# A long convolution with a gate: stores of a_u on two queues, sums in place, and another order of filter steps and halo copies

## The chip, the cores and the metric

The kernel runs on one core of a Trainium2 chip. The core has five engines, each with an instruction stream of its own: TensorE (PE) for matrix products, VectorE (DVE), ScalarE (ACT), GpSimd (POOL) and SyncE (SP), which here only issues DMAs. An engine runs its instructions in the order in which they were written and waits where data or a buffer isn't ready. What counts is the device time of one execution in microseconds (us): the median of three runs.

## What is computed

```
h = (relu(pos_emb @ w1) @ w2) * exp(-0.01 * n)          # filter, 12800 x 128
u = x * v                                               # 4 x 12800 x 128
y = irfft(rfft(u, 25600) * rfft(h, 25600))[:, :12800]   # a causal convolution along the sequence
z = x * y
gate = sigmoid(sum over k < 5 of conv_w[k] * z shifted by 4 - k)
out  = (gate * (z @ w_val)) @ w_out
```

Batch 4, sequence 12800, 128 channels, 64 features of the filter, all in float32 (some weights arrive as float64 and are narrowed on the chip).

## The kernel before, in words

The sequence is split as J * N1 * N2 = 2 * 100 * 64, and the transforms into a part over N1 and one over N2. The program has three stages, and two tensors in device memory lie between them: `a_u` (the transform of u over N1) and `c_y` (the product, transformed back over N2).

**Stage one** (L204 to L412) runs over the 64 values of n2. For each, `fetch` (L293) loads one tile of x and v, 100 rows of 8 KiB, as three DMAs of 64, 32 and 4 rows (the table `PARTS`). The tiles form a ring: four of the general buffers `ld0` to `ld3`, two of its own (`xv6`, `xv7`), and from the end of the filter's first part until 48 tiles are fetched also `ld4` and `ld5`. `product` (L313) multiplies x by v on DVE. For a pair of n2, `prep` (L320) then forms sums and differences: two operations of 1024 columns into the second half of the tile (L326, L327) and, for each n2, two of 512 into tiles `us` and `ud` of two buffers each (L334). PE multiplies them by the table `fsd` into `fp` (L379), ACT copies `fp` into `st` (L380, four buffers), and `st` goes to `a_u` as three stores: 64 and 32 rows from ACT's queue (L386), 4 rows from SP's, one n2 later (`flush`, L397). A pair's tiles are handed back to the ring by `release` inside `prep`, as soon as DVE has formed the sums of the odd n2, and `fetch` follows at once.

Between these steps a generator `filt` computes the filter's transform `ag`, in three parts: 16 times two steps that turn and multiply the positions (L228 to L242), 32 steps of PE with a copy by ACT (`ap`, L256 to L262), and 26 steps with a rotation by ACT and DVE (`fk`, L269 and L270), a product and a copy (L280, L282). A table of costs spreads the steps over the first 0.87 of stage one: the parts get 25.6, 28.8 and 22.9 of 77.3, which is 18.4, 20.7 and 16.5 n2.

Stage two (L440 to L540) reads `a_u`, multiplies by the filter and writes `c_y`. The change doesn't touch it.

**Stage three** runs over 32 groups of four n2, each a step `t` of four quarters `r`. In each quarter PE sums and turns rows of `c_y` (`sd`, L595; `tp`, L609); ACT copies `sd` into `sd_sb` (L602) and part of `tp` into `dif` (L611); DVE forms `yr` from `tp` and `dif` (L619, L620); POOL multiplies by x into `ext` (L622). For the group two behind, DVE adds one tap of the gate per quarter (`gt`, L637); the first tap is ACT's (`tap(t + 1, 0)`, L634, in the last quarter), the sigmoid too (`sg`, L641, last quarter), and, for every fourth group, also the copy of the last rows of the former `ext` into the new one (`fill_halo`, L576, last quarter; behind it the copy of `tails` for the last four groups of a half). PE's products `v_ps` and `o_ps` and ACT's copy `o_sb` (L664) complete the output.

**DMA counters.** The program gives every DMA that SP or ACT issues one of eight counters in turn, `DMAHW0` to `DMAHW7`, which count when it has landed; those of GpSimd have eight others, `DMASW0` to `DMASW7`. An issue waits until the DMA that had its counter before has landed. An engine that waits so holds everything behind it.

## Time and profile before

| | us |
|---|---|
| median of three runs | 1182.41 (1181.82 to 1184.42) |
| profiled execution | 1177.74 |
| its span, first to last instruction | 1176.0 |
| PE busy | 1027.8 (87%) |
| DVE busy | 992.6 (84%) |
| POOL busy | 679.7 (58%) |
| ACT busy | 622.6 (53%) |

All times of rows below come from the profiled execution. Issuing a DMA isn't counted as busy time, nor is waiting on a counter, so ACT's 53% leaves out what its queue of stores costs it. The mean granted clock of PE is 0.953. In a view by windows, each engine has the time it was busy in the window and, in brackets, its instructions; then come PE's clock, the share of the sixteen DMA engines that was busy, and GB/s. In a row of a group, the numbers behind the first bar are busy time and mean length (ns), behind the second the idle time ahead of these instructions and what ended it. ACTq and SPq are the DMA issues of ACT and SP.

### The profile page before, as it was taken

What the parts mean: (1) busy time and instruction counts of PE and PEld (TensorE: products, weight loads), DVE (VectorE), ACT (ScalarE), POOL (GpSimd) and SP (SyncE); (2) the same over time, 40 slices, a digit from 0 to 9 for tenths busy, and PEclk for the clock granted to TensorE, in tenths of its full rate; (3) what the DMA queues carried; (4) which work ended last, traced back from release to release, by engine and by line L of the source; (5) the groups of instructions that cost most, each with busy time, mean ns of one, the idle gap of its engine ahead of it and who ended that gap; (6) DMA issues with size and microseconds to landing.
All of it is one profiled execution on the core that took longest, in us unless ns stands there. A gap on an engine that the chain in (4) does not pass through costs nothing. (4 is left out here: it accounts for less than half of the span.)

```text
span 1176.0 us, 19204 instructions
## 1 busy us (share of the span) xinstructions
PE 1027.8 (87%) x6968; PEld 479.7 (41%) x6968; DVE 992.6 (84%) x1146; ACT 622.6 (53%) x1000; POOL 679.7 (58%) x290
## 2 busy tenths in 40 slices
PE   3767788967675799999999999988999999999986
PEld 1333345534341344444444444333444444444432
DVE  6678886659986799999999999718999999999996
ACT  1233366667774244444444444346676767676763
POOL 1000000000000699999999999928889898898880
PEclk9789889888989799999999999999999999999999
DMA  8889898875879789989999989787787777687622
GB/s 253 289 312 321 287 336 323 310 254 203 307 277 323 260 300 307 311 305 311 309 311 310 314 307 306 245 284 291 272 304 260 282 276 295 263 312 259 236 85 112
DMA packets 81384, 329.98 MB, mean 281 GB/s; under 512 B 11812, under 2 KB 13036, under 8 KB 62092
## 3 DMA queue, kind: packets, MB, share of 16 engines
q1 hardware_dynamic: 38512, 196.90, 50.1%
q10 hardware_dynamic: 42204, 130.02, 28.0%
q0 software_dynamic: 576, 1.84, 0.6%
q8 instruction: 57, 0.93, 0.3%
q14 instruction: 35, 0.29, 0.1%
HBM read 197.64 MB, written 131.07 MB: 280 GB/s over the span
## 5 line engine op out<-in xcount | busy, mean ns | idle before, releaser
L622 POOL TENSOR_TENSOR ext<-yr,xr 128x400 f32<-128x400 f32 x120 | 303.2, 2528 | 40.5 <-DVE yr L620 38.3
L637 DVE SCALAR_TENSOR_TENSOR gt<-ext,cw,gt 128x1600 f32<-128x1600 f32 x128 | 240.7, 1881 | 0.8 <-ACT gt L634 0.8
L380 ACT COPY st<-fp 128x1024 f32<-128x1024 f32 x128 | 128.7, 1027 | 174.9 <-PE fp L379 66.7
L484 ACT COPY c_sb<-c_ps 128x1024 f32<-128x1024 f32 x100 | 101.4, 1014 | 201.7 <-PE c_ps L479 194.8
L479 PE MATMUL c_ps<-va,ld 64*64 64x512 f32 x1600 | 194.1, 594 | 0.0
L468 DVE TENSOR_TENSOR va<-z_ps,h_sb 128x2048 f32<-128x2048 f32 x50 | 114.6, 2291 | 49.7 <-ACT h_sb L452 32.9
L513 POOL TENSOR_TENSOR va<-va,vb 128x1024 f32<-128x1024 f32 x50 | 118.6, 2373 | 45.6 <-DVE vb L468 45.5
L198 POOL DMA_DIRECT2D ld<-a_u x4 | 2.7, 683 | 240.6 <-DMA a_u<-st 240.6
L379 PE MATMUL fp<-us,fsd 64*128 64x512 f32 x256 | 87.2, 763 | 62.3 <-ACT st L380 35.5
L656 PE MATMUL o_ps<-gd,wout 128*128 128x400 f32 x256 | 112.4, 521 | 19.2 <-DVE gd L651 11.2
L595 PE MATMUL sd<-ld,inv 128*64 128x512 f32 x512 | 124.8, 605 | 2.0 <-ACT sd_sb L602 1.0
L522 POOL TENSOR_TENSOR va<-va,vb 128x1024 f32<-128x1024 f32 x50 | 119.6, 2392 | 0.0
L521 POOL TENSOR_TENSOR vc<-vc,vd 128x1024 f32<-128x1024 f32 x50 | 119.0, 2379 | 0.0
L462 PE MATMUL z_ps<-ld,ld 64*64 64x512 f32 x800 | 111.3, 606 | 7.4 <-DMA a_u<-st 4.0
L479 PEld LDWEIGHTS c_ps<-va,ld 64*64 64x64 f32 x1600 | 73.7, 135 | 101.2 <-issue 100.9
L602 ACT COPY sd_sb<-sd 128x512 f32<-128x512 f32 x128 | 76.1, 595 | 72.2 <-PE sd L595 55.5
L468 DVE TENSOR_TENSOR vb<-z_ps,h_sb 128x2048 f32<-128x2048 f32 x50 | 114.0, 2280 | 0.0
L646 PE MATMUL v_ps<-ext,wval 128*128 128x400 f32 x256 | 107.1, 500 | 0.0
L479 PE MATMUL c_ps<-vc,ld 64*64 64x512 f32 x800 | 98.2, 604 | 3.6 <-ACT c_sb L484 3.6
L609 PEld LDWEIGHTS tp<-ident,sd_sb 128*128 128x128 f32 x512 | 58.3, 140 | 75.8 <-PE sd L595 49.5
L609 PE MATMUL tp<-ident,sd_sb 128*128 128x128 f32 x512 | 79.9, 280 | 3.7 <-DVE yr L620 2.6
L619 DVE TENSOR_TENSOR yr<-tp,dif 128x204 f32<-128x204 f32 x128 | 45.9, 358 | 42.0 <-ACT dif L611 40.8
(85 smaller groups left out, 1560.6 us busy)
## 6 DMA issues: line engine op xcount, KB each, us to landing
c_y<-c_sb ACTq DMA_DIRECT2D x100, 512.0 KB
ld<-a_u SPq DMA_DIRECT2D x48, 1024.0 KB
a_u<-st ACTq DMA_DIRECT2D x64, 512.0 KB
ld<-c_y SPq DMA_DIRECT2D x64, 512.0 KB
xr<-in_xt_dram SPq DMA_DIRECT2D x32, 800.0 KB
out_dram<-o_sb ACTq DMA_DIRECT2D x32, 800.0 KB
ld<-in_xv_dram SPq DMA_DIRECT2D x46, 512.0 KB
a_u<-st ACTq DMA_DIRECT2D x64, 256.0 KB
```

The costliest lines, as they stand in the source:

```text
L380: nc.scalar.copy(out=st[:, c], in_=fp.rearrange("k j e -> k (j e)"))
L462: nc.tensor.matmul(out=z[half[h], c], lhsT=wk[half[c], 0, half[h]], rhs=a2[half[c], h, j], start=True, stop=True)
L468: nc.vector.tensor_tensor(out, z.rearrange("p (b d) -> p b d", d=D).unsqueeze(1).to_broadcast([128, n, B, D]), h_sb.unsqueeze(2).to_broadc ...
L479: nc.tensor.matmul(out=c_ps[half[m], h], lhsT=wk[half[h], 1 + c, half[m]], rhs=vt[half[h], c].rearrange("p b d -> p (b d)"), start=(i == 0 ...
L513: nc.gpsimd.tensor_tensor(va[:, 0:2], va[:, 0:2], vb[:, 0:2], op=ALU.add)
L521: nc.gpsimd.tensor_tensor(vc, vc, vd, op=ALU.add)
L522: nc.gpsimd.tensor_tensor(va[:, 2:4], va[:, 2:4], vb[:, 2:4], op=ALU.add)
L595: nc.tensor.matmul(out=sd[c * N2:(c + 1) * N2], lhsT=inv[:, c], rhs=rows_in[s, c][:, r * B * D:(r + 1) * B * D], start=True, stop=True)
L609: nc.tensor.transpose(out=tp[:, b], in_=t[:, b], identity=ident)
L622: nc.gpsimd.tensor_tensor(e[:, r0 + r], yr, xr, op=ALU.mult)
L637: nc.vector.scalar_tensor_tensor(gt, rows(t, k), cw[:, k:k + 1], gt, op0=ALU.mult, op1=ALU.add)
L656: nc.tensor.matmul(out=o_ps, lhsT=wout, rhs=gd, start=True, stop=True)
```

## The change

Five things are changed.

1. The 32-row and 4-row stores of `a_u`, and six loads of tables, are issued by GpSimd. ACT keeps the 64-row store.
2. The sums `us` and `ud` are written into the first half of the tile that they come from (for the even n2 its first, for the odd n2 its second 512 columns), where PE reads them.
3. The tiles of a pair are handed back, and the next fetched, behind the stores of the odd n2 and no longer in `prep`; the ring has one more tile, `xv8`, so it has seven to nine.
4. The filter's parts are due evenly over 15, 18 and 27 n2 from n2 = 2 on.
5. In stage three the first tap moves from the last quarter to the second, `fill_halo` to the first quarter of the next step, and the copy of `tails` to its third.

```
-        ring += [(6, p1.tile([128, 4 * BD], F32, name="xv6")), (7, p1.tile([128, 4 * BD], F32, name="xv7"))]
+        ring += [(6, p1.tile([128, 4 * BD], F32, name="xv6")), (7, p1.tile([128, 4 * BD], F32, name="xv7")),
+                 (8, p1.tile([128, 4 * BD], F32, name="xv8"))]
         for i, (_, t) in enumerate(ring):
-            (nc.vector, nc.gpsimd)[i in (2, 5)].memset(t, 0.0)
+            (nc.vector, nc.gpsimd)[i in (2, 4, 6)].memset(t, 0.0)
...
             for c, op in enumerate((ALU.add, ALU.subtract)):
-                w = p1.tile([128, BD], F32, name="us" if c == 0 else "ud", bufs=US)
+                w = srcs[c][:, 0, n % 2]
                 nc.vector.tensor_tensor(w, srcs[c][:, 1, 0], srcs[c][:, 1, 1], op=op)
                 out.append(w)
             if n % 2 == 1:
-                release()
-                fetch()
+                using.append(list(pair))
+                pair.clear()
                 if n + 1 < N2:
                     product(ahead.pop(0))
...
+        def release():
+            for i, t, _ in using.pop(0):
+                if i not in (4, 5) or fetched[0] < BACK:
+                    ring.append((i, t))
+            fetch()
...
                 if n == 8:
-                    nc.scalar.dma_start(out=dft, in_=t_dft)
+                    nc.gpsimd.dma_start(out=dft, in_=t_dft)
...
-                for k0, k, step, p0 in PARTS[:2]:
-                    nc.scalar.dma_start(out=dst[k0:k0 + k], in_=src[p0:p0 + step * (k - 1) + 1:step])
+                for eng, (k0, k, step, p0) in zip((nc.scalar, nc.gpsimd), PARTS):
+                    eng.dma_start(out=dst[k0:k0 + k], in_=src[p0:p0 + step * (k - 1) + 1:step])
+                if n % 2 == 1:
+                    release()
                 rest.append((dst, src))
...
                 k0, k, step, p0 = PARTS[2]
-                nc.sync.dma_start(out=dst[k0:k0 + k], in_=src[p0:p0 + step * (k - 1) + 1:step])
+                nc.gpsimd.dma_start(out=dst[k0:k0 + k], in_=src[p0:p0 + step * (k - 1) + 1:step])
...
-        FS = 0.87
+        spans = [(J * N2 // 4, 15), (FO // 2, 18), (N1 // 4 + 1, 27)]
+        due = [2 + sum(w for _, w in spans[:k]) + w * i / n for k, (n, w) in enumerate(spans) for i in range(n)]
+        sig, fil = signal(), filt()
         with tc.manual_schedule():
-            cost = [0.7, 0.9] * (J * N2 // 8) + [0.9] * (FO // 2) + [0.4] + [0.9] * (N1 // 4)
-            spent, steps = 0.0, iter(cost)
-            for i in range(n_sig):
+            for i in range(2 * N2):
                 next(sig, None)
-                while spent < sum(cost) and spent * n_sig * FS <= (i + 1) * sum(cost):
+                while due and due[0] <= i / 2:
                     next(fil, None)
-                    spent += next(steps, sum(cost))
+                    due.pop(0)
...
-                    if r == R - 1 and 0 <= t + 1 < NT:
-                        tap(t + 1, 0)
...
+                    if r == 0 and halo:
+                        fill_halo(*halo)
+                    if r == 1 and 0 <= t + 1 < NT:
+                        tap(t + 1, 0)
+                    if r == 2 and halo:
+                        if halo[1] == NG // EG - 1:
+                            nc.scalar.copy(out=exts[halo][:, EG * R:], in_=tails[halo[0]])
+                        halo = None
                     if r == R - 1 and 0 <= t < NT:
                         sigmoid(t)
-                    if r == R - 1 and s < NT and g % EG == 0:
-                        fill_halo(j, g // EG)
+                if s < NT and g % EG == 0:
+                    halo = j, g // EG
```

How the instructions stand then is seen on three engines. First SP in the middle of stage one, before: bursts of six loads (`ld_..` and `xv_..` are tiles of the ring) and behind each two 4-row stores that wait for ACT.

```order
L298 DMA xv_101<-in_xv_dram 64x2048 [waits DMAHW7_49,DVE_49]
L298 DMA xv_101<-in_xv_dram 32x2048 [waits DMAHW0_49]
L298 DMA xv_101<-in_xv_dram 4x2048 [waits DMAHW1_49]
L298 DMA xv_102<-in_xv_dram 64x2048 [waits DMAHW3_49]
L298 DMA xv_102<-in_xv_dram 32x2048 [waits DMAHW5_49]
L298 DMA xv_102<-in_xv_dram 4x2048 [waits DMAHW6_49]
L397 DMA a_u<-st 4x2048 [waits DMAHW7_49,Activation_49]
L397 DMA a_u<-st 4x2048 [waits DMAHW0_49,Activation_49]
```

And SP with the change, at the same place: loads alone, whose first waits for PE too.

```order
L299 DMA xv_102<-in_xv_dram 64x2048 [waits DMAHW4_49,DVE_49,PE_49]
L299 DMA xv_102<-in_xv_dram 32x2048 [waits DMAHW5_49]
L299 DMA xv_102<-in_xv_dram 4x2048 [waits DMAHW6_49]
L299 DMA xv_103<-in_xv_dram 64x2048 [waits DMAHW7_49]
L299 DMA xv_103<-in_xv_dram 32x2048 [waits DMAHW1_49]
L299 DMA xv_103<-in_xv_dram 4x2048 [waits DMAHW2_49]
```

The stores have left SP's queue, and the loads take six counters of eight in every pair. Second, ACT in the filter's third part, before (`fk`, `ag` and `gp` belong to the filter):

```order
L380 COPY st<-fp 128x1024 [waits PE_49]
L386 DMA a_u<-st 64x2048 [waits DMAHW7_49,Activation_49]
L386 DMA a_u<-st 32x2048 [waits DMAHW0_49]
L380 COPY st<-fp 128x1024 [waits DMAHW1_49,PE_49]
L269 ACTIVATE fk<-dft,tw 128x128 [waits DVE_49]
L269 ACTIVATE fk<-dft,tw 128x128 x3
L282 COPY ag<-gp 128x512 [waits PE_49]
```

With the change the same stretch of ACT reads:

```order
L385 DMA a_u<-st 64x2048 [waits DMAHW6_49,Activation_49]
L379 COPY st<-fp 128x1024 [waits DMASW4_49,DMASW1_49,PE_49]
L379 COPY st<-fp 128x1024 [waits PE_49]
L269 ACTIVATE fk<-dft,tw 128x128 [waits DVE_49]
L269 ACTIVATE fk<-dft,tw 128x128 x3
L282 COPY ag<-gp 128x512 [waits PE_49]
L385 DMA a_u<-st 64x2048 [waits DMAHW3_49,Activation_49]
```

One store per n2 is left on ACT; its counter alternates between two that the loads of the pair don't use. The copy into `st` now waits for GpSimd's stores of four n2 earlier. GpSimd's own queue at the end of stage one, with the change (`ld_76` is a buffer of stage two, L198 its load):

```order
L385 DMA a_u<-st 32x2048 [waits DMASW3_49,Activation_49]
L398 DMA a_u<-st 4x2048 [waits DMASW4_49]
L198 DMA ld_76<-a_u 56x2x1024 [waits DMAHW2_49,DMAHW0_49,DMAHW7_49,DMASW5_49,PE_49]
L198 DMA ld_76<-a_u 56x2x1024 [waits DMASW6_49,PE_49]
L385 DMA a_u<-st 32x2048 [waits DMASW7_49,Activation_49]
L398 DMA a_u<-st 4x2048 [waits DMASW0_49]
L398 DMA a_u<-st 4x2048 [waits DMASW1_49]
```

Before, only the rows of L198 stood there. Third, ACT in stage three around a halo copy, before (L588 copies the halo):

```order
L634 ACTIVATE gt<-ext,cw 128x1600
L602 COPY sd_sb<-sd 128x512
L641 ACTIVATE sg<-gt 128x1600
L588 COPY ext<-ext 128x1600
L611 COPY dif<-tp_6359 128x204
L664 COPY o_sb<-o_ps 128x400
```

With the change (L587 copies the halo):

```order
L638 ACTIVATE sg<-gt 128x1600
L608 COPY dif<-tp_6674 128x204
L661 COPY o_sb<-o_ps 128x400
L599 COPY sd_sb<-sd 128x512
L587 COPY ext<-ext 128x1600
L608 COPY dif<-tp_6702 128x204
L661 COPY o_sb<-o_ps 128x400
L664 DMA out_dram<-o_sb 128x1600
L599 COPY sd_sb<-sd 128x512
L631 ACTIVATE gt<-ext,cw 128x1600
```

Between any two of the three large pieces now stands a round of the small copies `dif`, `o_sb` and `sd_sb`.

More of the change, by code (lines that the diff above doesn't have):

```diff
@@ L302, in fetch @@
                 fetched[0] += 1
-        def release():
-            for i, t, _ in pair:
-                if i not in (4, 5) or fetched[0] < BACK:
-                    ring.append((i, t))
-            pair.clear()
         def halves(t):
@@ L316, in product @@
             pair.append((*it, u))
-        pair = []
+        pair, using = [], []
         def prep(n):
@@ L358, in signal @@
                         raw = p1.tile(list(dst.shape), mybir.dt.int64, name=f"raw{len(raws)}")
-                        nc.scalar.dma_start(out=raw, in_=src)
+                        nc.gpsimd.dma_start(out=raw, in_=src)
                         raws.append((dst, raw))
@@ L588, in fill_halo @@
                 nc.scalar.copy(out=e[:, 0:HALO], in_=exts[j, q - 1][:, EG * R:])
-            if q == NG // EG - 1:
-                nc.scalar.copy(out=e[:, EG * R:], in_=tails[j])
         def y_sum(s, r):
@@ L672, in tile_longconv_gate @@
         AHEAD3, NT, LAG = 3, len(groups), 2
[L673 removed]
+        y_run, gd_last, o_last, halo = [], None, None, None
         with tc.manual_schedule():
```

8 lines of the change are left out of this document (2 added, 6 removed).

## The prediction

> **What bounds the kernel now.** I cut the span into its three stages and the first stage into stretches, with the view of busy time by windows.
>
> ```profile
> core 0: us, PE busy (x) PEld busy (x) DVE busy (x) ACT busy (x) POOL busy (x), PEclk, DMA share, GB/s
> 0.00:365.00 365.00, 266.10 (x1384) 143.33 (x1384) 283.59 (x426) 187.45 (x277) 8.81 (x10) 0.87 0.82 291
> 715.00:1176.00 461.00, 426.18 (x2084) 193.09 (x2076) 405.07 (x537) 289.45 (x497) 364.34 (x148) 0.99 0.69 254
> ...
> 20.00:120.00 100.00, 74.19 (x314) 37.20 (x316) 73.42 (x94) 32.43 (x33) 1.80 (x1) 0.85 0.88 305
> 120.00:140.00 20.00, 13.77 (x84) 7.86 (x82) 17.47 (x31) 4.87 (x5) 1.80 (x1) 0.90 0.75 270
> 140.00:240.00 100.00, 88.66 (x598) 51.59 (x600) 72.94 (x102) 63.59 (x68) 0.00 (x0) 0.88 0.88 319
> 240.00:340.00 100.00, 71.42 (x328) 40.19 (x326) 80.84 (x158) 71.82 (x153) 0.00 (x0) 0.85 0.68 252
> 340.00:380.00 40.00, 24.16 (x94) 8.40 (x92) 30.27 (x38) 21.20 (x26) 2.73 (x4) 0.95 0.92 330
> ```
>
> In stage one no engine is full, and the transfers nearly are: 305 to 330 GB/s at a share of 0.88 to 0.92, except in two stretches. From 120 to 140 us they fall to 270 and from 240 to 340, where the filter's third part runs, to 252 GB/s. Those two are the slack. The waits of that stage say why it isn't used (columns: total us, times, longest).
>
> ```profile
> ACT st L380 <- DMA ld<-in_xv_dram: 47.9, 12, 9.0
> ACT st L380 <- DMA a_u<-st: 33.6, 11, 5.5
> ACT st L380 <- DMA xv<-in_xv_dram: 7.6, 4, 3.2
> ...
> DVE ud L334 <- PE fp L379: 19.5, 14, 2.6
> DVE fk L270 <- ACT fk L269: 15.1, 13, 5.7
> DVE us L334 <- PE fp L379: 9.4, 7, 1.8
> ```
>
> ACT's copy into `st` has no use for x and v, and yet stands 47.9 + 7.6 us behind their loads. It is the DMA issue in front of it that waits, as the timeline of ACT and of SP shows (start, us, engine):
>
> ```profile
> 133.19 6.92 ACTq L386 DMA_DIRECT2D a_u<-st  x2
> 140.20 1.01 ACT L380 COPY st<-fp 128x1024 f32<-128x1024 f32 x1 [7.04 <-DMA ld<-in_xv_dram]
> ...
> 254.18 4.29 SPq L298 DMA_DIRECT2D ld<-in_xv_dram  x6
> 258.99 13.27 SPq L397 DMA_DIRECT2D a_u<-st  x4
> 280.33 1.74 SPq L298 DMA_DIRECT2D ld<-in_xv_dram  x3
> ```
>
> Two stores hold ACT for 6.92 us. SP and ACT share eight landing counters, and a DMA is issued when the one eight before it has landed (the listings above). Per pair of n2 there are six loads and six stores, so a store comes to wait for loads just sent. On SP, four 4-row stores stand from 258.99 to 272.3 between two bursts of loads.
>
> Stage three is bound by DVE, which runs without gaps but for one kind:
>
> ```profile
> L637 DVE SCALAR_TENSOR_TENSOR gt<-ext,cw,gt 128x1600 f32<-128x1600 f32 x109 | 204.1, 1872 | 0.0
> L619 DVE TENSOR_TENSOR yr<-tp,dif 128x204 f32<-128x204 f32 x108 | 38.6, 358 | 10.1 <-ACT dif L611 10.1
> ...
> 875.49 1.64 ACT L634 ACTIVATE gt<-ext,cw 128x1600 f32<-128x1600 f32 x1
> 877.03 0.59 ACT L602 COPY sd_sb<-sd 128x512 f32<-128x512 f32 x1
> 877.49 1.56 ACT L641 ACTIVATE sg<-gt 128x1600 f32<-128x1600 f32 x1
> 878.93 1.53 ACT L588 COPY ext<-ext 128x1600 f32<-128x1600 f32 x1
> 880.35 0.35 ACT L611 COPY dif<-tp 128x204 f32<-128x204 f32 x1
> ...
> 881.43 0.38 ACT L611 COPY dif<-tp 128x204 f32<-128x204 f32 x1
> ...
> 884.17 1.87 DVE L637 SCALAR_TENSOR_TENSOR gt<-ext,cw,gt 128x1600 f32<-128x1600 f32 x1
> ...
> 887.00 1.87 DVE L637 SCALAR_TENSOR_TENSOR gt<-ext,cw,gt 128x1600 f32<-128x1600 f32 x1
> ```
>
> From 815 to 1130 us DVE idles 10.1 us in all, each time behind ACT's `dif`. ACT then has the first tap, the sigmoid and the halo one after the other, from 875.49 on, and `dif` comes only at 880.35. Once ACT is late, a round of its three small copies takes 881.43 - 880.35 = 1.08 us; a round of DVE takes 887.00 - 884.17 = 2.83.
>
> **The change, part by part.** *Stage one, the queues.* Of twelve DMAs per pair of n2, eight stay on the shared counters: six loads and ACT's two 64-row stores. By the listing a store then takes the counter of a store one pair earlier, and SP has no store in front of its loads. GpSimd gets the 32-row and 4-row stores, 128 in all, and six table loads. It was busy for 8.81 of the first 365 us, so its issue is hidden if it costs what the four rows of GpSimd's own loads show:
>
> ```profile
> L198 POOL DMA_DIRECT2D ld<-a_u x4: 639/642/808, 351.6 to 366.0; - x4
> DMA to landing us min/median/max: 5.8/9.0/12.0
> ```
>
> 134 issues of 0.64 us are 86 us beside some 365. So I let the waits of ACT on loads go, and ask what is late next. In the stretch from 240 to 340 us the groups by line give it:
>
> ```profile
> L380 ACT COPY st<-fp 128x1024 f32<-128x1024 f32 x32 | 32.3, 1018 | 25.8 <-PE fp L379 10.4 <-DMA ld<-in_xv_dram 6.6 <-DMA a_u<-st 3.9
> L270 DVE SCALAR_TENSOR_TENSOR fk<-dft,tw,fk 128x128 f32<-128x128 f32 x96 | 28.3, 349 | 17.4 <-ACT fk L269 14.7 <-PE gp L280 2.7
> ```
>
> 32 copies are 16 n2, so one takes 100/16 = 6.25 us. DVE works 80.84/16 = 5.05 us of it, six `fk` of 28.3/96 = 0.295 us each. *The filter's third part* now has 27 n2 for its 100 `fk`, 3.7 per n2: DVE needs 5.05 - 2.3 x 0.295 = 4.4 us. An n2 moves 100 rows of 8 KiB in and as many out, 1.64 MB; at 312 GB/s, the mean of 305 and 319, it takes 5.25 us. So the transfers become the bound there. The stretch of 100 us shrinks to 100 x 252/312 = 80.8 us, **-19.2 us**, and that from 120 to 140 to 17.3, **-2.7 us**. Bounds: nothing gained, and 330 GB/s throughout, -23.6 and -3.6.
>
> *The second part* has 32 steps in 18 n2. In the window from 140 to 240:
>
> ```profile
> L380 ACT COPY st<-fp 128x1024 f32<-128x1024 f32 x38 | 39.5, 1053 | 42.0 <-DMA a_u<-st 16.6 <-DMA ld<-in_xv_dram 15.4 <-PE fp L379 5.9
> L256 PE MATMUL ap<-fwd,g_sb 100*64 100x200 f32 x224 | 36.7, 408 | 0.0
> ```
>
> 19 n2 carry 224/8 = 28 steps, 1.47 per n2, with PE busy 88.66 us, 4.67 per n2; at 1.78 PE comes to about 5.2. That is level with the transfers, without room for a bubble: **+2 us** (from 0, if ACT's freed time closes the bubbles, to +5). The first part, 18.4 n2 long by the old table and 15 now, stays under the transfers that carry its table of positions: 0.
>
> *What is given back at the end.* The last n2 now run without filter work:
>
> ```profile
> 367.69 1.93 ACT L380 COPY st<-fp 128x1024 f32<-128x1024 f32 x2 [1.43 <-PE fp L379]
> ...
> 371.13 1.93 ACT L380 COPY st<-fp 128x1024 f32<-128x1024 f32 x2 [1.50 <-PE fp L379]
> ...
> 385.10 0.59 ACT L452 COPY h_sb<-c_ps 128x512 f32<-128x512 f32 x1 [4.89 <-DMA a_u<-st]
> ```
>
> That is 3.4 us per n2; with the filter reaching n2 61 it is some 4.9. Three n2 after the last load: **+4.5 us** (0 to 10). Stage two starts when the last store has landed. GpSimd sends three stores at the end where ACT and SP sent theirs side by side: two more issues of 0.64 us and I take **+1.5 us** (0 to 6, half of the 12.0 us above).
>
> *Sums in place, one more tile.* The 28.9 us of DVE's waits on `fp` go; DVE isn't the bound of stage one, so this is inside the terms above. In exchange a pair of tiles is freed only when PE has read its sums, some 1.5 n2 later in the order; the additional tile pays one of them. 0, from -3 to +5. The seventh memset runs on GpSimd beside DVE's four: 0.
>
> Stage one: -19.2 - 2.7 + 2 + 4.5 + 1.5 = **-14 us** (from -29 to +6).
>
> *Stage three.* The first tap moves to the second quarter of a step, the halo to the first of the next, the tail's copy to the third. The rows of ACT above give each about 1.5 us; a quarter of a step is one round of DVE, 2.83 us, and 1.08 + 1.5 fits into it. No quarter holds two large pieces any more: the 10.1 us go, **-10 us** (0 to -12, as the first halo lies ahead of the window).
>
> **Sum.** The profiled execution took 1177.74 us, its span and 1.7 around it: 1177.74 - 14 - 10 = 1153.7. The median of the runs stands 4.67 us over it; so the forecast is **1158 us**.
>
> The Trainium skill, DMA: Bandwidth & Descriptors, section Issuing engines are not separate DMA queues, says that transfers started by SP, ACT or GpSimd end on the same sixteen engines and that several issuers save only the time of issuing. By that rule alone stage one gains nothing where the transfers are full; the rows at 0.88 to 0.92 agree, those at 0.68 and 0.75 leave room, and the rule is the first rival below.
>
> **The rivals.**
>
> *The transfers were the bound all along.* Loads and stores that ran late at 252 GB/s were caught up at 330 afterwards; three queues only share the same rate. For it: 330 GB/s right behind the slow stretch, and 319 before it. Against it: 252 over 100 us is far below, with engines waiting on each other. Stage one then gains 2 us, stage three its 10: 1177.74 - 12 + 4.67 = 1170.
>
> *Stage one at its best rate.* With 330 GB/s and nothing given back, -27 and -10: 1145.
>
> *Stage three's stall stays.* 1.08 + 1.5 against 2.83 us is tight, with waits between the copies, and ahead of the last four groups of each half all four quarters are filled. Then only the -14 are left: 1168.
>
> *Slower: the stores of GpSimd land late.* `st` has four buffers. The 4-row store of n is queued behind the 32-row one of n + 1, so a buffer is back one n2, a copy of 2 us and a landing L after it was filled, and four n2 must cover that: a pace P = (2 + L)/3. Up to the largest landing seen, 12.0 us, P is 4.7 and hidden. From L = 15 us it decides, as P then reaches the 365/64 = 5.7 us of now; at 17 us it is 6.3 and costs 64 x 0.6 = 38 us, which makes 1177.74 + 38 - 10 + 4.67 = 1210. For it: those were four transfers, not 134. Against it: they were of 448 KB, these are of 256 and 32.
>
> The Trainium skill, SBUF — State Buffer, section Who interferes with whom, says that DVE's copies, casts and tensor-scalar operations in their fast modes keep GpSimd from writing the descriptors of its DMAs, and tensor-tensor operations not. By that rule L would grow beside DVE; here DVE's work in stage one is nearly all tensor-tensor, and no run so far shows it.
>
> **Chances.** Forecast 0.49 (1150 to 1166); transfers 0.20 (1166 to 1178); best rate 0.13 (1138 to 1150); stall stays 0.06; slower 0.12. The range reaches from 1141 to 1178: it takes in the bounds on both sides and leaves out the slower case and the end of the best one. A difference within 0.2% can't be told from none: 1180.0 to 1184.8. Faster 0.85, same 0.03 (the late end of the transfers' case), slower 0.12.
>
> **What would show it.** Right: from 240 to 340 us at 300 GB/s or more; no wait of `st` on loads; stage two starting near 371 in place of 385; no idle time of DVE before `yr`. Wrong: a wait of `st` on `a_u<-st` above 34 us (late stores), DMA issues of GpSimd far over 0.64 us, DVE waiting for loads (tiles freed too late), PE full from the 17th to the 35th n2 at a slower pace, or gaps that only move to another quarter in stage three.

## The result, and the profile after

| | before | changed |
|---|---|---|
| median of the runs taken side by side, us | 1183.41 | 1133.13 (1132.23 to 1134.35) |
| ratio | | 0.9574 (0.9552 to 0.9596) |
| profiled execution, us | 1177.74 | 1133.82 |
| its span, us | 1176.0 | 1132.0 |

The change gains 4.3%, about 50 us where 24 were forecast. 1133 lies under the lower end of the range, 1141, and also under the time of the case "stage one at its best rate".

First the view by windows, for the changed kernel, in the same stretches as before:

```profile
core 0: us, PE busy (x) PEld busy (x) DVE busy (x) ACT busy (x) POOL busy (x), PEclk, DMA share, GB/s
...
20.00:120.00 100.00, 72.94 (x310) 37.19 (x308) 74.19 (x94) 32.45 (x33) 21.09 (x37) 0.81 0.87 305
120.00:140.00 20.00, 16.57 (x102) 9.47 (x100) 18.19 (x31) 9.11 (x10) 6.91 (x8) 0.82 0.86 313
140.00:240.00 100.00, 92.47 (x662) 57.33 (x660) 83.06 (x130) 77.73 (x101) 24.15 (x44) 0.97 0.95 358
240.00:340.00 100.00, 74.81 (x328) 39.01 (x326) 96.36 (x162) 72.83 (x140) 23.19 (x42) 0.88 0.81 304
```

The slow stretch from 240 to 340 us went from 252 to 304 GB/s, and DVE is busy there for 96.36 us of 100: it has become the bound. From 140 to 240 us, which the prediction took as full at 319 GB/s, the rate is now 358, and PE is busy for 92.47 us at a granted clock of 0.97 in place of 0.88. From 20 to 120 us nothing moved. These windows stand at fixed times, and the changed kernel is further on in its work at each of them; the parts themselves are compared below.

ACT's copies into `st` in the same two stretches (140 to 240, then 240 to 340), from the groups by line:

```profile
L379 ACT COPY st<-fp 128x1024 f32<-128x1024 f32 x43 | 44.6, 1053 | 12.8 <-PE fp L378 11.5 <-ACT st L379 1.2
L379 ACT COPY st<-fp 128x1024 f32<-128x1024 f32 x42 | 41.9, 1015 | 27.2 <-PE fp L378 22.1 <-PE gp L280 5.0
```

43 copies where there were 38, and 42 where there were 32; no wait on a DMA is left in either. Over all of stage one from 20 us on, ACT's waits on DMAs ahead of these copies, 47.9 + 33.6 + 7.6 = 89.1 us before, are down to two:

```profile
ACT st L379 <- PE fp L378: 105.4, 83, 12.5
ACT st L379 <- DMA xv<-in_xv_dram: 7.5, 1, 7.5
ACT st L379 <- DMA a_u<-st: 6.5, 1, 6.5
```

The timeline of ACT in the second part shows what that looks like:

```profile
184.88 1.06 ACT L379 COPY st<-fp 128x1024 f32<-128x1024 f32 x1 [0.20 <-PE fp L378]
186.31 0.87 ACT L262 COPY ag<-ap 128x400 f32<-128x400 f32 x1 [0.37 <-PE ap L260]
187.38 1.07 ACT L379 COPY st<-fp 128x1024 f32<-128x1024 f32 x1 [0.20 <-PE fp L378]
188.80 0.88 ACT L262 COPY ag<-ap 128x400 f32<-128x400 f32 x1 [0.36 <-PE ap L260]
188.86 0.46 ACTq L385 DMA_DIRECT2D a_u<-st  x1
```

Two copies into `st` take 4.99 us (189.87, where the next pair of rows begins, less 184.88), ACT waits for PE alone, and a store's issue takes 0.46 us. The time of an n2 here is that of PE.

Where the stages begin and end, by the first and last start of their instructions (of the changed kernel):

```profile
L379 ACT COPY st<-fp x128: 992/1012/1110, 19.1 to 344.9; 128x1024 f32<-128x1024 f32 x128
L451 ACT COPY h_sb<-c_ps x50: 585/586/588, 356.5 to 722.5; 128x512 f32<-128x512 f32 x50
L592 PEld LDWEIGHTS sd<-ld,inv x512: 132/136/138, 744.5 to 1087.5; 128*64 128x64 f32 x171
```

and of the kernel before:

```profile
L380 ACT COPY st<-fp x128: 992/1014/1162, 18.8 to 379.2; 128x1024 f32<-128x1024 f32 x128
L452 ACT COPY h_sb<-c_ps x50: 586/586/587, 385.1 to 751.9; 128x512 f32<-128x512 f32 x50
L595 PEld LDWEIGHTS sd<-ld,inv x512: 132/136/137, 776.6 to 1131.4; 128*64 128x64 f32 x171
```

| stretch | before | changed | difference | predicted |
|---|---|---|---|---|
| start to the last copy into `st` | 379.2 | 344.9 | -34.3 | -15.4 |
| from there to the first `h_sb` | 5.9 | 11.6 | +5.7 | +1.5 |
| first to last `h_sb` (stage two) | 366.8 | 366.0 | -0.8 | 0 |
| from there to the first `sd` | 24.7 | 22.0 | -2.7 | 0 |
| first to last `sd` (stage three) | 354.8 | 343.0 | -11.8 | -10 |
| from there to the end | 44.6 | 44.5 | -0.1 | 0 |

The column sums to -44.0, which is the difference of the spans. The other 6 us of the medians' 50 are in the runs: those of the kernel before lay between 1174.6 and 1189.7 in all comparisons here, and its profiled execution, at 1177.74, near the lower end; those of the changed kernel lay between 1130.2 and 1134.4.

### The profile page after: what moved, and what is told of

The parts are those of the page before. It is cut to its first block, busy times and chain, and to the rows that moved or that the text cites. A ratio compares the mean times of both kernels' runs of the same rounds, so it can differ in the third digit from the quotient of the medians.

```text
span 1132.0 us, 19317 instructions
## 1 busy us (share of the span) xinstructions
PE 1013.6 (90%) x6968; PEld 480.6 (42%) x6968; DVE 991.4 (88%) x1146; ACT 626.3 (55%) x1000; POOL 757.8 (67%) x425
## 4 chain that ended last, share of the span: by engine, by line
PE 36%; DVE 23%; issue 9%; ACT 4%; DMA 3%; ACTq 0%; SPq 0%; POOL 0%; POOLq 0%; DVEq 0%
PE c_ps L478 23%; DVE gt L634 11%; PE z_ps L461 8%; DVE gd L648 6%; DVE yr L616 3%; DVE yr L617 2%; ACT st L379 2%; PE c_ps L445 2%; PE fp L378 2%; ACT fk L269 1%; DMA c_y<-c_sb 1%; PE gp L280 1%; DMA xr<-in_xt_dram 1%; DMA a_u<-st 1%; ACT ag L282 1%
## 5 line engine op out<-in xcount | busy, mean ns | idle before, releaser
L385 POOL DMA_DIRECT2D a_u<-st x64 | 34.3, 537 | 257.5 <-ACT st L379 209.9
L378 PE MATMUL fp<-ld,fsd 64*128 64x512 f32 x320 | 100.3, 725 | 46.0 <-DVE ld L329 17.0
L653 PE MATMUL o_ps<-gd,wout 128*128 128x400 f32 x256 | 111.6, 517 | 11.4 <-DVE gd L648 11.2
L599 ACT COPY sd_sb<-sd 128x512 f32<-128x512 f32 x128 | 75.9, 593 | 44.8 <-PE sd L592 33.6
L648 DVE TENSOR_TENSOR gd<-v_ps,sg 128x400 f32<-128x400 f32 x128 | 71.8, 561 | 3.1 <-PE v_ps L643 1.9
```

Source lines behind the costliest of these rows:

```text
L378: nc.tensor.matmul(out=fp[:, j], lhsT=fsd[h, c], rhs=both[c][h], start=True, stop=True)
L648: nc.vector.tensor_tensor(gd, v_ps, gate_sg[t][:, r * ROW:(r + 1) * ROW], op=ALU.mult)
```

## The experiments

All ratios are to the kernel before, run on the same chip between the runs of the others.

### Stage three by itself

Only the part of the change in stage three, on the kernel before:

```
+                    if r == 0 and halo:
+                        fill_halo(*halo)
+                    if r == 1 and 0 <= t + 1 < NT:
+                        tap(t + 1, 0)
...
```

> The kernel before with the change of stage three alone (first tap in the second quarter, halo in the first quarter of the next step, tails in the third); stage one as before. What the two traces show: from the first to the last sd 354.8 us before and 343.0 with the whole change, -11.8; from the last z_ps to the first sd 21.6 and 18.8, -2.8. Theory (the stage's stall is gone by the new order alone, and is worth what the trace shows): 0.990 of the kernel before (about 1171.5 us), first to last sd 343 us, no idle time of DVE before yr on dif. Rival (part of the 11.8 us comes from other things, such as which buffers stage one hands on): 1175 us or more, with DVE gaps left.

Measured: 1170.0 us, 0.9898 (0.987 to 0.9925). From the first to the last `sd` it took 781.1 to 1124.4, 343.3 us. The groups by line, from 820 to 1120 us of this run and from 785 to 1086 us of the changed kernel:

```profile
L617 DVE TENSOR_TENSOR yr<-tp,dif 128x204 f32<-128x204 f32 x107 | 50.1, 468 | 0.0
```

```profile
L616 DVE TENSOR_TENSOR yr<-tp,dif 128x204 f32<-128x204 f32 x107 | 37.9, 354 | 0.0
```

No idle time is left ahead of `yr`, where there were 10.1 us. The theory held. Two things are open. One `yr` takes 468 ns in this run and 354 in the changed kernel, without a difference in the stage's time (the other operations of DVE are longer by as much, and as many run in the same time, so their rows overlap); why was not tried. And the 2.7 us between the last `h_sb` and the first `sd` are not from this part: here that stretch takes 26.0 us, against 24.7 before, and over all runs it varied from 20.4 to 26.0 us with no tie to a part of the change.

### Which part of the change made stage one faster

Each part alone on the kernel before, and the changed kernel without its queues. Stores and table loads back where they were:

```
-                for eng, (k0, k, step, p0) in zip((nc.scalar, nc.gpsimd), PARTS):
+                for eng, (k0, k, step, p0) in zip((nc.scalar, nc.scalar), PARTS):
...
-                nc.gpsimd.dma_start(out=dst[k0:k0 + k], ...)
+                nc.sync.dma_start(out=dst[k0:k0 + k], ...)
```

> The changed kernel with every store and table load of stage one back on the queue that it had before: 64 and 32 rows on ACT's, 4 rows on SP's. Left of the change are sums in place with the ninth tile, the filter's parts and stage three. Theory Q (the prediction's: DMA issues that wait for loads held stage one, and GpSimd's queue takes the wait away): the waits of st on loads come back, 30 us or more from 20 to 350 us, the rate from 240 to 340 us falls under 285 GB/s, and at least 15 us of the 37 us that stage one gained are given back: 1148 us or more. Theory F (the filter's even parts made the gain): within 6 us of the changed kernel, 1139 us or less. Theory S (the sums in place freed DVE and PE): the same as by F.

The opposite, the two new queues and nothing else:

```
-                for k0, k, step, p0 in PARTS[:2]:
-                    nc.scalar.dma_start(...)
+                for eng, (k0, k, step, p0) in zip((nc.scalar, nc.gpsimd), PARTS):
+                    eng.dma_start(...)
...
-                nc.sync.dma_start(out=dst[k0:k0 + k], ...)
+                nc.gpsimd.dma_start(out=dst[k0:k0 + k], ...)
```

> The kernel before with the 32-row and 4-row stores and the six table loads on GpSimd's queue, and nothing else of the change. Theory Q: the waits of st on loads (55.5 us) go, the rate from 240 to 340 us rises from 252 GB/s to 290 or more, and 15 to 25 us are gained: 1158 to 1168 us. Theories F and S: the slow stretch stays, as DVE's rotations and its waits on fp stay; less than 6 us gained, 1177 us or more.

The filter's spans alone:

```
-        FS = 0.87
+        spans = [(J * N2 // 4, 15), (FO // 2, 18), (N1 // 4 + 1, 27)]
...
```

> The kernel before with the filter's parts due over 15, 18 and 27 n2 from n2 = 2 on, and nothing else of the change. Theory F: the third part's n2 come at 5.3 us or less in place of 6.25, the rate from 240 to 340 us is 290 GB/s or more, 15 to 25 us are gained: 1158 to 1168 us. Theory Q: the stores and loads still wait for one another; less than 6 us gained, 1177 us or more. Theory S: likewise.

Sums in place, the later release and the ninth tile alone:

```
-                w = p1.tile([128, BD], F32, name="us" if c == 0 else "ud", bufs=US)
+                w = srcs[c][:, 0, n % 2]
...
+                if n % 2 == 1:
+                    release()
```

> The kernel before with sums in place, tiles handed back behind the stores of the odd n2 and the ninth tile, and nothing else of the change. The prediction put this at 0, from -3 to +5. Theory S: DVE's 28.9 us of waits on fp were in the way of the rotations and of the next sums; 10 us or more gained, 1173 us or less. Theories Q and F: within 5 us of the kernel before, 1178 to 1188.

| kernel | us | ratio | last `st`, us |
|---|---|---|---|
| queues alone | 1141.7 | 0.9671 (0.9592 to 0.9749) | 337.4 |
| filter's spans alone | 1170.3 | 0.9912 (0.9886 to 0.9938) | 380.2 |
| sums in place alone | 1172.8 | 0.9934 (0.9906 to 0.9963) | 379.1 |
| changed, stores back | 1153.3 | 0.9749 (0.9686 to 0.9813) | 369.7 |

The queues alone are worth 3.3%, 38 us against the kernel before that ran beside them and more than the 15 to 25 of the theory that favoured them, and bring the last copy into `st` from 379.2 to 337.4 us: further than the whole change does, at 344.9. Taking them out of the change gives back 1.8%, as that theory had it. One of its signs failed there, though: from 240 to 340 us the kernel with the stores back moves 313 GB/s, not under 285, and loses its time earlier (284 GB/s from 20 to 120 us, 325 from 140 to 240); the waits of `st` on x and v are 25.8 us, not 30.

The other two parts bring 0.9 and 0.7%, 9 and 7 us, and in their profiles the last `st` has not moved. By the time alone, sums in place would just fit theory S (1173 or less), and the spans fit neither theory. But the profiled executions of the two lie only 3.0 and 3.6 us under that of the kernel before, and the stretch from the last `h_sb` to the first `sd` alone is 4.1 us shorter in both; the rest of their gain shows in no trace.

The windows of the kernel with the queues alone:

```profile
20.00:120.00 100.00, 75.63 (x326) 37.85 (x326) 78.90 (x100) 35.13 (x35) 24.95 (x42) 0.86 0.93 334
120.00:140.00 20.00, 14.25 (x93) 8.12 (x92) 18.43 (x34) 7.52 (x8) 4.14 (x6) 0.93 0.64 235
140.00:240.00 100.00, 93.68 (x664) 57.34 (x664) 83.88 (x126) 79.54 (x104) 24.45 (x44) 0.97 0.96 367
240.00:340.00 100.00, 69.10 (x344) 34.76 (x344) 91.08 (x160) 73.70 (x140) 26.67 (x47) 0.97 0.84 298
```

334 and 367 GB/s stand where 305 and 319 had looked like full transfers. From 240 to 340 us it comes to 298 without any change of the filter's schedule; but that window no longer holds the same work, as the last `fk` starts at 306.9 us here and at 343.0 before. So here is the filter's third part itself, about from its first `fk` to its last: before, with the queues alone, with the spans alone, and changed.

```profile
248.00:343.00 95.00, 71.04 (x318) 40.18 (x320) 80.27 (x158) 70.36 (x155) 0.00 (x0) 0.85 0.67 248
222.00:306.00 84.00, 60.45 (x316) 34.11 (x318) 77.96 (x155) 68.85 (x153) 16.67 (x30) 0.98 0.82 294
233.00:369.00 136.00, 96.85 (x396) 50.11 (x396) 115.14 (x198) 88.25 (x175) 2.72 (x4) 0.84 0.81 290
214.00:334.00 120.00, 88.41 (x389) 46.61 (x388) 113.42 (x195) 87.80 (x173) 27.77 (x50) 0.88 0.87 326
```

ACT makes 31, 31, 51 and 51 copies into `st` in them, two per n2, so an n2 takes 95/15.5 = 6.13 us, 84/15.5 = 5.42, 136/25.5 = 5.33 and 120/25.5 = 4.71. Each of the two speeds up the slow part by itself, and together they do more. But with the spans alone the stage gets no shorter: 293 and 300 GB/s from 20 to 120 and from 140 to 240 us, in place of 305 and 319, take back what its third part gains.

If the queues do this alone, the rest of stage one may cost something. Two kernels: queues and stage three without the rest (the diffs of those two parts together), and the changed kernel with the old schedule of the filter.

> The kernel before with two parts of the change alone: the stores and table loads on GpSimd's queue, and the new order of stage three; us and ud in tiles of their own, eight tiles in the ring, the filter's old schedule. If the two parts add up: 1141.7 - 12.9 = 1129 us, below the changed kernel's 1133.1; the last copy into st came at 337.4 us with the queues alone and at 344.9 in the changed kernel. Rival: the slower runs of the queues alone (1136 to 1147) show that this order is near another bound, and the time is 1133 us or more.

```
-        spans = [(J * N2 // 4, 15), (FO // 2, 18), (N1 // 4 + 1, 27)]
+        FS = 0.87
...
```

> The changed kernel with the filter's old schedule (all steps by their costs over 0.87 of the stage); queues, sums in place, nine tiles and stage three as changed. Theory X (with the loads free, the filter's even parts cost more at the front, where 15 n2 take all of the first part, than they save in the third): 1130 us or less, last copy into st before 341 us. Theory F (the even parts still pay): 1137 us or more, and the third part's n2 at 5.6 us or more.

The first: 1131.2 us, 0.9567 (0.952 to 0.9615), last `st` at 338.3, between its two expectations. The second: 1128.4 us, 0.9541 (0.9492 to 0.959), last `st` at 335.4, as theory X had it. The changed kernel was then run once more:

> The changed kernel itself, to stand beside the two others of this call on one chip. If the filter's even spans cost what the last copies into st show (344.9 us with them, 335.4 without), it is 4 to 6 us slower than the kernel with the old schedule was (1128.4): 1132 to 1134; by the rival the two are the same, 1128 to 1130.

Measured: 1131.4 us, 0.9562 (0.9535 to 0.9589), between the two expectations. So the whole of sums in place, ninth tile and even spans adds nothing that can be told from queues and stage three; the profiles say that the even spans take back what the sums bring (last `st` 344.9 and 341.8 with them, 335.4 without; from 20 to 120 us, where their first part is packed into 15 n2, 305 and 321 GB/s against 335), but the intervals of the times overlap, and that point stays a reading of the profiles.

### Why the queues matter so much

Three edits of the changed kernel on one question: does it matter which of the small transfers goes where? The 32-row stores back on ACT, the 4-row stores on ACT, and the 4-row loads on GpSimd:

```
-                for eng, (k0, k, step, p0) in zip((nc.scalar, nc.gpsimd), PARTS):
+                for eng, (k0, k, step, p0) in zip((nc.scalar, nc.scalar), PARTS):
```

> The changed kernel with the 32-row stores of a_u back on ACT's queue; GpSimd keeps the 4-row stores, so ten DMAs of a pair of n2 go by the eight shared counters in place of eight. Theory A (what counts is that no DMA issue stands behind loads just sent; the prediction's queues): ACT's copy into st waits for loads again, 10 us or more in sum, stage one 5 to 15 us longer, 1140 to 1148 us, and the next kernel of this call, which also has ten, the same. Theory B (what counts is the way the 4-row DMAs go: those of SP and ACT load few of the sixteen DMA engines, those of GpSimd others, and the rate from 140 to 240 us rose from 319 to 358 GB/s at shares of 0.88 and 0.95 by that): the rate there stays at 345 GB/s or more and the time is within 4 us of the changed kernel, 1130 to 1137. The Trainium skill, DMA: Bandwidth & Descriptors, section Why a DMA increments its semaphore by 16 and not by 1, says that a DMA of SP or ACT over k engines takes the k lowest of the sixteen, one of GpSimd k consecutive ones from a place that moves on; theory B is what this would do here.

```
-                nc.gpsimd.dma_start(out=dst[k0:k0 + k], ...)
+                nc.scalar.dma_start(out=dst[k0:k0 + k], ...)
```

> The changed kernel with the 4-row stores of a_u on ACT's queue in place of GpSimd's, one n2 later as before; GpSimd keeps the 32-row stores. Ten DMAs of a pair of n2 go by the shared counters, as in the kernel before it in this call. Theory A (queues and counters alone): the same as that kernel, 1140 to 1148 us, or less, as the 4-row store is the smaller one. Theory B (few of the DMA engines carry all 4-row DMAs): per n2 there are 200 rows; with both 4-row pieces on the same four engines those carry 14 rows against a mean of 12.5, so no more than 12.5/14 = 0.893 of the time of all engines can be used (0.88 was measured before), 13.25 with the stores spread, 0.943 (0.95 was measured after). So the share from 140 to 240 us falls back to 0.90 or less and the rate to 340 GB/s or less; 16 n2 that took 74.5 us then take 78 or more, and the time is 5 to 10 us above the changed kernel, 1138 to 1144, and above that of the 32-row stores on ACT.

```
-                    nc.sync.dma_start(out=t[...], in_=xv[n, k0:k0 + k])
+                    (nc.gpsimd if k == 4 else nc.sync).dma_start(out=t[...], in_=xv[n, k0:k0 + k])
```

> The changed kernel with the 4-row loads of x and v on GpSimd's queue too; SP keeps those of 64 and 32 rows. Theory A (queues): GpSimd's loads stand behind stores that wait for ACT's copy into st, the last four rows of a tile come late, DVE waits for them; 0 to 15 us slower, 1133 to 1148. Theory B (few engines carry the 4-row DMAs): no engine carries more than 12.5 rows per n2 in the mean, the share may go above 0.95 where transfers bound the stage, 20 to 120 us above all (0.87 at 305 GB/s in the changed kernel): there 325 GB/s or more, and 3 to 8 us less in all, 1125 to 1130. From 140 to 240 us PE is busy for 92.5 of 100 us in the changed kernel, so no more than 2 us can come from there.

Measured, in this order: 1135.3 us, 0.9616 (0.9562 to 0.9669); 1137.2 us, 0.9621 (0.9566 to 0.9675); 1132.9 us, 0.9579 (0.9519 to 0.9638). Theory B met the first (350 GB/s from 140 to 240 us) and fell with the second. With both 4-row pieces on SP and ACT the window reads

```profile
140.00:240.00 100.00, 89.06 (x626) 54.52 (x624) 82.45 (x128) 76.92 (x103) 11.68 (x22) 0.96 0.94 354
```

354 GB/s at a share of 0.94, where that theory set 0.893 as the most; and the 4-row loads on GpSimd brought nothing (320 GB/s from 20 to 120 us, where that theory asked for 325 or more). What the Trainium skill, DMA: Bandwidth & Descriptors, section Why a DMA increments its semaphore by 16 and not by 1, says of the lowest engines may be so; as a limit on the rate, these runs don't show it. Theory A fell in its size. The waits came back: `st` stands 46.1 us behind DMAs in the first kernel and 33.6 in the second, 21.4 and 24.7 of it behind loads. But ten DMAs on the shared counters cost 2 to 4 us over eight, with intervals that overlap, not 5 to 15.

So twelve were tried with no store on SP, and ten in the kernel before, where the 4-row stores alone go to GpSimd:

```
-                for eng, (k0, k, step, p0) in zip((nc.scalar, nc.gpsimd), PARTS):
+                for eng, (k0, k, step, p0) in zip((nc.scalar, nc.scalar), PARTS):
...
-                nc.gpsimd.dma_start(out=dst[k0:k0 + k], ...)
+                nc.scalar.dma_start(out=dst[k0:k0 + k], ...)
```

> The changed kernel with all three stores of each n2 on ACT's queue, the 4-row one an n2 later as before; the six table loads stay with GpSimd, and SP's queue keeps loads alone. Theory O (order of SP's queue: the 4-row stores, which wait for ACT's copy of the n2 before, stood in front of the next loads; moving them anywhere off SP is what counts, since 1153.3 us with them on SP became 1135.3 when they alone stood with GpSimd): 1134 to 1142 us. Theory C (the eight shared counters: twelve DMAs of a pair on eight counters make ACT wait for loads, wherever the stores stand): 1147 us or more, with 30 us of waits of st on DMAs.

```
-                nc.sync.dma_start(out=dst[k0:k0 + k], ...)
+                nc.gpsimd.dma_start(out=dst[k0:k0 + k], ...)
```

> The kernel before with the 4-row stores on GpSimd's queue in place of SP's, and nothing else. All three moves together (32 rows, 4 rows, tables) gave 1141.7 us. Theory O: SP's loads are free of stores, two thirds or more of those 38 to 41 us come by this move alone, 1142 to 1155 us. Theory C: two DMAs of twelve leave the shared counters, four come with the 32-row ones; a third or less, 1167 us or more, with ACT's waits on loads still 30 us or more.

Measured: 1163.8 us, 0.9843 (0.9789 to 0.9896), and 1162.3 us, 0.9841 (0.9785 to 0.9898). The first is as theory C had it and against theory O: SP has loads alone there, and the time is worse than with the 4-row stores on SP (1153.3). Its groups of waits (stage one from 20 us on) show the loads again:

```profile
ACT st L379 <- DMA xv<-in_xv_dram: 31.8, 13, 9.2
ACT st L379 <- DMA ld<-in_xv_dram: 27.1, 12, 4.4
ACT st L379 <- issue: 9.0, 4, 2.6
ACT st L379 <- DMA a_u<-st: 8.5, 2, 5.6
```

and its timeline of ACT how it comes about (two stores of an n2, then the 4-row store of the n2 before):

```profile
188.81 1.17 ACTq L385 DMA_DIRECT2D a_u<-st  x2
191.98 0.51 ACTq L398 DMA_DIRECT2D a_u<-st  x1
192.59 1.01 ACT L379 COPY st<-fp 128x1024 f32<-128x1024 f32 x1 [2.36 <-DMA ld<-in_xv_dram]
```

The two issues end at 189.98; the third store goes out only at 191.98 and holds the copy, whose wait the trace puts down to a load. The second result lies between the two expectations: a bit under half of what both stores together bring. Last, the same relief from the other side, loads in place of stores:

```
-                    nc.sync.dma_start(out=t[...], in_=xv[n, k0:k0 + k])
+                    (nc.sync if k == 64 else nc.gpsimd).dma_start(out=t[...], in_=xv[n, k0:k0 + k])
```

> The kernel before with the 32-row and 4-row loads of x and v on GpSimd's queue; all stores stay on ACT's and SP's. Eight DMAs of a pair of n2 are then left on the shared counters, two loads and six stores, as many as with the stores moved. Theory C (what counts is how many DMAs share the eight counters): as with the queues alone, 1141.7 us, within 10 us: 1135 to 1152. Theory I (what counts is that ACT and SP issue stores at all): 1165 us or more, with ACT's waits of st on a_u 30 us or more. In between, both.

Measured: 1153.5 us, 0.9774 (0.9736 to 0.9812); 347 GB/s from 140 to 240 us, last `st` at 354.4; just above the range of theory C and far under theory I's. That is some two thirds of what the stores bring (2.3% beside 3.3), with all stores where they were: most of the gain needs no store on GpSimd. Its waits name what may hold the rest:

```profile
POOL ld L298 <- DVE ud L334: 171.3, 18, 22.0
POOL xv L298 <- DVE ud L334: 71.6, 8, 14.2
...
ACT st L380 <- DMA a_u<-st: 24.2, 8, 9.4
```

GpSimd's loads stand until DVE has freed their tile, and the stores that stayed still make ACT wait, 24.2 us. And is eight the end of it? With the 64-row stores on GpSimd too, six are left:

```
+                for eng, (k0, k, step, p0) in zip((nc.gpsimd, nc.gpsimd), PARTS):
```

> The kernel with the old filter schedule (changed otherwise), with the 64-row stores on GpSimd's queue as well: ACT issues no store, six DMAs of a pair of n2 are left on the shared counters. Theory C (fewer on the counters and less on ACT's queue go on paying): the last st at 332 us or sooner and 1125 us or less. Rival (at eight the waits are gone, 9 us of st on DMAs are left, and PE and DVE are busy for some 90 of 100 us; GpSimd's three issues per n2 and its eight counters become the next wait): 1128 us or more, st waiting for a_u.

Measured: 1127.5 us, 0.9523 (0.9489 to 0.9556), between the two expectations, beside 1128.4 and 0.9541 with eight; the waits of `st` on `a_u` came to 18.7 us in the profiled execution, the slowest of its runs. Nothing that can be told from eight.

By the number of DMAs of a pair of n2 on the shared counters, from runs of the kernel before and of the changed one; in brackets all waits of `st` on DMAs in stage one from 20 us on, from the traces:

| on the counters | kernel before, us | changed kernel, us |
|---|---|---|
| 12 | 1179.6 to 1184.2 (89.1) | 4 rows on SP 1153.3 (56.6), all on ACT 1163.8 (69.4) |
| 10 | 1162.3 (41.3) | 32 rows on ACT 1135.3 (46.1), 4 rows on ACT 1137.2 (33.6) |
| 8 | stores moved 1141.7 (19.4), loads moved 1153.5 (40.0) | 1131.4 (13.1), 1133.1 (14.0) |
| 6 | - | 4-row loads moved too 1132.9 (12.5) |

In both columns the time falls as that number falls: down to ten in the changed kernel, down to eight in the one before; what lies below can't be told apart. The number alone doesn't set the time: at twelve and at eight two places of the same number of DMAs lie 10 and 12 us apart. Nor is a wait its cost: at ten in the changed kernel 46.1 and 33.6 us of waits are left and cost some 2 to 4 us, which is within the noise. That kernel hands its tiles back later, has one more of them and spreads the filter's steps evenly; which of these lets it bear the waits was not tried. One more thing these runs don't take apart: whoever leaves the shared counters here also gets onto a third queue of transfers, GpSimd's, with eight counters of its own. A kernel with fewer DMAs on the counters and no third queue was not tried.

### The end of stage one

The stores of the last two n2 back on ACT and SP, on the kernel with the old schedule:

```
-                for eng, (k0, k, step, p0) in zip((nc.scalar, nc.gpsimd), PARTS):
+                for eng, (k0, k, step, p0) in zip((nc.scalar, nc.scalar if n >= N2 - 2 else nc.gpsimd), PARTS):
...
+                rest.append((nc.sync if n >= N2 - 2 else nc.gpsimd, dst, src))
```

> The kernel with the old filter schedule (1128.4 us, the changed kernel otherwise), with the stores of the last two n2 back on ACT's queue (32 rows) and SP's (4 rows). Theory T (GpSimd's stores at the end are what stage two waits for: from the last st to the first h_sb 11.2 us there, 5.9 in the kernel before): that distance falls to 7 us or less and the time by 3 to 5 us, 1123 to 1126. Rival (the last 64-row stores and the loads of a_u that follow take that long anyway): the distance stays at 10 us or more and the time at 1127 or more.

Measured: 1126.3 us, 0.9536 (0.9504 to 0.9568), and from the last `st` at 336.9 to the first `h_sb` at 347.0 still 10.1 us. The theory fell. The issues of GpSimd's early loads of `a_u`, from the view of their line, told more. Before, they went out from 351.6 to 366.0 us (the row is in the prediction); in the changed kernel:

```profile
L198 POOL DMA_DIRECT2D ld<-a_u x4: 659/680/695, 338.6 to 345.8; - x4
...
  ACT h_sb L451: 10.5, 1
...
DMA to landing us min/median/max: 5.9/7.3/9.4
```

So before, the last of them went out 13.2 us ahead of the last copy into `st`; with the change it goes out 0.9 us behind it, and ACT's first `h_sb` waits 10.5 us for these loads. GpSimd's queue now holds stores that wait for ACT, and these loads stand behind them. So they were put on SP's queue, behind the last loads of x and v:

```
-                        load_a(0, part, nc.gpsimd)
+                        load_a(0, part)
...
-                        load_a(1, part, nc.gpsimd)
+                        load_a(1, part)
```

> The kernel with the old filter schedule (changed otherwise), with the four early loads of a_u for stage two on SP's queue, behind the last loads of x and v, in place of GpSimd's, where they stand behind stores that wait for ACT. Theory E (stage two starts late because these loads go out late, and land 7 to 9 us after): from the last st to the first h_sb 7 us or less in place of 11.2, and 3 to 5 us gained on the kernel with the old filter schedule: 1123 to 1126 us. Rival (the loads wait for their buffers or for the last stores wherever they stand): 10 us or more, 1127 or more.

Measured: 1123.4 us, 0.949 (0.9464 to 0.9517). Stage two starts 343.5 - 336.9 = 6.6 us behind the last `st`:

```profile
L379 ACT COPY st<-fp x128: 1012/1014/1333, 18.8 to 336.9; 128x1024 f32<-128x1024 f32 x128
...
L453 ACT COPY h_sb<-c_ps x50: 585/586/587, 343.5 to 711.3; 128x512 f32<-128x512 f32 x50
```

This version beats both kernels: its interval and that of the changed kernel run beside it (0.9535 to 0.9589) don't meet. It has the old schedule of the filter too, and against that schedule without this move (0.9492 to 0.959) the intervals overlap. So what the four loads are worth is read from the traces: from the last `st` to the first `h_sb` 6.6 us in place of 11.2.

### Other spans

On the kernel with the last stores back on ACT and SP:

```
-        FS = 0.87
+        spans = [(J * N2 // 4, 18), (FO // 2, 19), (N1 // 4 + 1, 22)]
...
```

> As the kernel before it in this call, with the filter's parts due evenly over 18, 19 and 22 n2 from n2 = 0.5 on. Theory P (each part is bound by another engine: the first by the transfers with its tables, the second by PE, busy 92 of 100 us, the third by DVE, at 5.3 to 6.3 us per n2; a longer third part takes DVE's load down, and the first keeps its length): 3 to 8 us less than that kernel, 1117 to 1122. Rival (the bound is the sum of the stage's transfers, 365 GB/s whatever the spans): no more than 2 us of difference.

Measured: 1129.6 us, 0.9573 (0.9543 to 0.9604), against 1126.3 for the old schedule beside it. The theory fell: nothing was gained, and the last `st` came at 341.4 in place of 336.9 (the intervals of the times overlap). A longer third part does not pay for itself here, though DVE is the busiest engine there; what it costs at the other places was not followed further.

## Why the prediction was wrong

**The step that failed** is the size of *Stage one, the queues*: the waits of `st` on loads were seen, and let go, but their worth was taken from the two slow stretches only. Everywhere else 305 to 330 GB/s at a share of 0.88 to 0.92 was read as transfers that are nearly full. They were not: 358 GB/s in the changed kernel and 367 with the queues alone. The same waits that were quoted as the reason for the slow stretch held the fast ones too; in the window from 140 to 240 us ACT stood 16.6 + 15.4 us behind DMAs in the very row that the prediction showed. The term that this mis-sized most is that of the second part, +2 us, measured -9.9.

Term by term:

- *The second part* was set at **+2 us**, as PE was level with the transfers. From its first copy of `ag` to its last, before and changed, it reads

```profile
131.00:243.00 112.00, 97.82 (x666) 56.86 (x664) 84.84 (x118) 67.99 (x73) 0.00 (x0) 0.89 0.86 311
129.00:212.00 83.00, 83.00 (x638) 53.08 (x636) 70.83 (x105) 63.67 (x66) 18.88 (x34) 0.97 0.93 346
```

  with 41 and 35 copies into `st`: 112/20.5 = 5.46 and 83/17.5 = 4.74 us per n2. The 19 n2 of the window from 140 to 240 us come to 90.1 us in place of 100: -9.9. Both halves of the reason were off. The transfers went on to 346 GB/s; and PE, full as foreseen, needs 4.74 us and not 5.2, as its granted clock was 0.97 where it had been 0.89 (5.2 x 0.89/0.97 = 4.8, an estimate). Why the clock rose isn't shown: with the queues alone it was 0.97 both with PE busy for 93.68 us of 100 and with 69.10. This one term is 11.9 of the 14.6 us by which stage one was missed; the others below nearly cancel.
- *The slow stretch*, **-19.2**: at 4.71 us per n2 its 16 n2 take 75.3 us in place of 100, -24.7, just beyond its bounds. It isn't bound by the transfers at 5.25 us, as predicted: they move 326 GB/s. DVE is busy for 113.42 of 120 us there, 4.45 per n2, which is what the prediction had worked out for it. And the reason given, fewer `fk` per n2, is one of two: the queues alone do about as much (5.42 us per n2, the spans alone 5.33, in place of 6.13).
- *What is given back at the end*, +4.5, and the stretch from 120 to 140 us, -2.7: the sum of all terms up to the last `st` leaves about +0.3 for the two, against +1.8.
- *The stage's end*, **+1.5**, measured +5.7, within its bounds of 0 to 6. The cause was not among the ones named. The rows of GpSimd's queue ahead of the prediction show the loads of `a_u` between two stores that wait for ACT; that they would go out some 14 us later, against the stage's end, was not read from them.
- *Sums in place, one more tile*, 0: alone they bring 0.7%, with the queues nothing that can be told.
- *Stage three*, **-10**, measured -11.8 in the profile and 1.0% (0.75 to 1.3) alone: right, by the mechanism given.
- *Stage two and what follows it* were put at nothing and took 3.6 us less (-0.8, -2.7 and -0.1); no part of the change was found to do it.
- *From profile to median*, **+4.67**, was carried over from the kernel before. The changed kernel's median stands 0.7 us under its profiled execution: 5.4 us of the miss.

With these two terms as predicted the time would be 1177.74 - 28.6 - 11.8 + 4.67 = 1142 us, still inside the range, at its fast end. That range was also narrower than its terms: their bounds add up to about -30 and +26 for stage one, not to -29 and +6.

Of the rivals, *the transfers were the bound all along* is refuted by the 38 us from queues alone; the section of the Trainium skill cited there (DMA: Bandwidth & Descriptors, Issuing engines are not separate DMA queues), by which several issuers would save only the time of issuing, does not cover a kernel in which the issuers wait for each other's transfers. *Stores of GpSimd land late* did not come about:

```profile
a_u<-st POOLq DMA_DIRECT2D x64, 256.0 KB, 6.0
...
a_u<-st POOLq DMA_DIRECT2D x64, 32.0 KB, 6.3
```

L is 6.0 and 6.3 us at the median, far under the 15 from which it would decide. By the Trainium skill, SBUF — State Buffer, section Who interferes with whom, DVE's tensor-tensor work leaves GpSimd's DMAs alone, and these landings don't speak against it. *Stage three's stall stays* is refuted by the idle time of 0.0. *Stage one at its best rate* was the nearest, and still took 330 GB/s for the most.

## What to carry to other kernels

A high mean rate of the transfers is no proof that they are the bound as long as an engine that issues them is seen waiting for one of them: count the DMAs in a round against the counters that they share, and try one queue more before tuning the order of the compute. What a wait costs, only a run tells: taking away 70 us of waits gained 38 us in one kernel (89.1 to 19.4), and 32 us more of them cost some 2 us in another (14.0 to 46.1). When DMAs move to another queue, list everything that already stands in that queue and when it must go out; here four loads of the next stage held its start up by 4.6 us (11.2 and 6.6). And an estimate that scales an engine's time should ask whether its clock was granted in full when that time was taken.

## What was not expected of the hardware

Transfers at a mean share of 0.88 of the sixteen engines, steady over 100 us, could still be raised to 0.96 (319 to 367 GB/s), with the same kinds of transfers. The kernel before varied by 15 us between runs (1174.6 to 1189.7), the changed one by 4 (1130.2 to 1134.4); the run with queues alone, by 11 (1136.1 to 1147.3), so the wider spread isn't tied to twelve DMAs on the counters, and its cause stays open.
